# ScalarE clears two output tiles inside expert 0's branch, and the hint for the next branch is given twice per pair of tiles

## The chip, the cores and the metric

The program runs on one core of one Trainium2 chip. The metric is device time in microseconds (us) of that core, from the start to the end of one launch; the kernel before has a median of 473.15 us over three runs (471.51 to 475.03). The profiled execution is one more run of the same program. Its own time was 470.77 us; the span from its first to its last recorded instruction was 469.1 us.

Engine names follow the profile: PE is TensorE (matmuls), PEld its weight loads, ACT is ScalarE, DVE is VectorE, POOL is GpSimd, SP is SyncE. A name with a q behind it (PEq, ACTq, PEldq) is an engine's sequencer, which handles waits, registers, branches and hints.

## The reference

Two blocks are chained. The first is a retention recurrence over 4 batches, 8 heads, 768 steps and width 64; its output, laid out as 3072 tokens of 512 numbers, is the input of the second. The second is a mixture of 8 experts with one expert per token:

```python
logits = x @ w_gate
expert_idx = np.argmax(logits, axis=1)
gate_w = probs[np.arange(N), expert_idx]
...
for e in range(E):
    ...
    h = np.maximum(x_sorted[lo:hi] @ w1[e], 0.0)
    y_sorted[lo:hi] = h @ w2[e]
y = y_sorted[inv_perm]
return (gate_w[:, None] * y).astype(np.float32)
```

w1 of an expert is 512 by 1024, w2 is 1024 by 512, all in 32-bit floats. How many tokens an expert gets is known only once the gate has been computed on the chip.

## The kernel before

**The two phases.** The attention phase takes about the first 130 us of the span. It runs in 24 steps of 128 tokens, places each token in a list of its expert as it goes, and stores the rows in DRAM. It closes with the first two tiles of 128 rows of expert 0, worked on early: layer 1 of these 256 rows, and then layer 2 by `pair` (L341), a product of block matrices with 7 products instead of 8. Each of the 7 products is 4 matmuls in the source and 8 matmul records in the profile (a 32-bit matmul is recorded twice). Then the expert phase runs the experts 0 to 7 in a Python loop (L900), fully unrolled.

**The branch of an expert.** How many rows an expert has is rounded up to a multiple of 8, and each possible count has code of its own: a `tc.Switch` (L933) with 33 arms, of which one is run. PE and ACT take this branch at every expert, DVE from expert 1 on. The arm of expert 0 or 1 holds layer 1 (`layer_one`, L912, with `layer1`, L220) and layer 2 of the tiles that `pair` does not do. Layer 1 is eight groups of four matmuls into four PSUM banks in turn; ACT moves each group out with a Relu (L225), and PE may begin group 4 only when ACT has emptied the bank of group 0. Layer 2 is `layer2` (L227), its matmuls are L236 and ACT's evictions L241 to L244. From expert 2 on, layer 1 is done by `quarters1` (L291, matmuls L303), again by 7 products.

**The work between two branches.** For the experts 1 to 7, what follows the arm is straight code: `pair` on the first two tiles (matmuls L349, ACT L364 and L376, DVE L355), the scatter of the output rows and the gather of later input rows by POOL (L392, L166), weight loads by SP (L150, L155), and transposes of the next expert's rows by DVE (L209).

**The hint.** The target of a branch is computed at run time, so the kernel announces it: `fetch_ahead` (L410) gives PE and ACT a hint of which arm comes next. `pair` calls it as `then()` after its third product of seven (L370); in expert 0 and in the early pair other calls do so. At the head of each arm the framework puts a hint of its own for the jump out of the arm (recorded at L933). The arithmetic of a branch and its COMPARE_BRANCH are recorded at L989, the hint given by `fetch_ahead` at L411.

**The clearing.** Expert 0's rows beyond its real count are scattered as well (to rows out of bounds, which are dropped), so the first two tiles of `o2[0]` have to hold something. ACT clears them by two activations with scale 0.0 (L887), 128 by 512 each, placed ahead of the expert loop. `o2` lies in memory that the attention phase has used before; the first instruction that writes there waits for the last reader of each engine, among them DVE's last L355 of the early pair.

**What sets the order.** From L700 on, the order on every engine is the order of the source (`manual_schedule`), and each engine's queue is worked off in that order.

Of the kernel before, what the change touches and what calls it, by code (L numbers as in the profile page):

```python
# [17 lines left out]
AF = mybir.ActivationFunctionType  # L18
# [3 lines left out]
P = 128  # L22
# [24 lines left out]
def middle(ap, n):  # L47

    dims = [list(d) for d in ap.ap]
    return bass.AP(tensor=ap.tensor, offset=ap.offset, ap=[dims[0], [0, n]] + dims[1:])  # L50
# [3 lines left out]
def kernel(  # L54
# [11 lines left out]
    nc = tc.nc  # L66
    B, H, S, D = q.shape
    N, DM = out.shape
# [18 lines left out]
    def ps(tag, bufs, name):  # L87
        return psum.tile([P, 512], F32, tag=tag, name=name, bufs=bufs)
# [9 lines left out]
    ident = const.tile([P, P], F32, tag="ident", name="ident")  # L98
# [115 lines left out]
    def turn(xs, xT, tiles, which=range(Q * Q)):  # L214
        for _ in turns(xs, xT, tiles, which):
            pass
# [124 lines left out]
    def pair(hT, w2t, hs, ws, o, gate, then, tile_of, spare=lambda n: None, tags=None,  # L341
             late=False):

        ya, yb, yc, yd = ((ps(*tag, "yp") if tags else acc8[tag])[:, 0:DH] for tag in tags or (4, 5, 2, 3))
        g = [gate[:, i : i + 1] for i in range(2)]

        def product(y, a, b, start):
            for f in range(FH):
                nc.tensor.matmul(y, lhsT=a[:, f, :], rhs=b[:, f, :], start=start and f == 0, stop=f == FH - 1,  # L349
                                 skip_group_check=True)  # L350

        def part(name, y, i, plus):

            to = tile_of(name) if isinstance(name, str) else name
            nc.vector.scalar_tensor_tensor(out=to, in0=y, scalar=g[i], in1=plus, op0=ALU.mult, op1=ALU.add)  # L355
            return to

        A = lambda i, j: hT[:, ts(j, FH), ts(i, P)]
        B = lambda j, k: w2t[:, 0, ts(j, FH), ts(k, DH)]
        S, T = [None] + hs, [None] + ws  # L360
        m1 = [tile_of(f"m1{i}") for i in range(2)]
        product(ya, A(0, 0), B(0, 0), True)
        for i in range(2):
            nc.scalar.activation(out=m1[i], in_=ya, func=AF.Copy, scale=g[i])  # L364
        product(yb, S[2], T[2], True)
        u20, u21 = (part(f"u2{i}", yb, i, m1[i]) for i in range(2))
        spare(4)
        product(yd, S[3], T[3], True)
        u3 = part("u3", yd, 1, u21)
        then()  # L370
        spare(7)
        product(yc, S[1], T[1], True)
        part(o[:, 1, DH:DM], yc, 1, u3)
        spare(5)
        product(ya, A(0, 1), B(1, 0), False)
        nc.scalar.activation(out=o[:, 0, 0:DH], in_=ya, func=AF.Copy, scale=g[0])  # L376
        product(yd, A(1, 1), T[4], False)
        if not late:
            part(o[:, 1, 0:DH], yd, 1, u21)
        product(yc, S[4], B(1, 1), False)  # L380
        if not late:
            part(o[:, 0, DH:DM], yc, 0, u20)

        def rest():
            part(o[:, 1, 0:DH], yd, 1, u21)
            part(o[:, 0, DH:DM], yc, 0, u20)

        return rest
# [14 lines left out]
    HALF = EARLY // P  # L403
    ARMS = MOST - LEAST + 1

    def regs(e):
        return {g: nc.engines[g].value_load(arm[0:1, e : e + 1], min_val=0, max_val=ARMS - 1)
                for g in ((PE, ACT) if e < 1 else (PE, ACT, DVE))}

    def fetch_ahead(which, e):  # L410
        tc.switch_hint({g: which[g] for g in (PE, ACT)}, ARMS, label=f"job{e}")  # L411
# [381 lines left out]
    o2 = [keep2.tile([P, TC, DM], F32, tag=f"o{i}", name=f"o{i}") for i in range(2)]  # L793
# [89 lines left out]
            scatter(o2[E % 2], odst[:, ts(j, TC)], range(TC))  # L883

    if True:
        for h in range(HALF):
            nc.scalar.activation(out=o2[0][:, h, :].rearrange("p (a b) -> p a b", b=P), in_=middle(ident[:, :], DM // P),  # L887
                                 func=AF.Copy, scale=0.0)
        acc8.extend(ps(tag, n, f"p{i}") for i, (tag, n) in enumerate((("sc", 2), ("sc", 2), ("lg", 1)) + (("tr", 3),) * 3 + (("y", 2),) * 2))
        xT, xTn, rest = xTa, xT1, None  # L890
        s3 = [keep2.tile([P, 2, F // 2], F32, tag=f"s{i}", name=f"s{i}", bufs=1) for i in range(3)]
        T = [keep2.tile([P, 2, W // 2], F32, tag=f"t{i}", name=f"t{i}", bufs=1) for i in range(4)]
        hs = [keep2.tile([P, FH * P], F32, tag=f"hs{i}", name=f"hs{i}", bufs=1) for i in range(4)]
        ws = [keep2.tile([P, FH * DH], F32, tag=f"ws{i}", name=f"ws{i}", bufs=1) for i in range(4)]
        temps = [[keep2.tile([P, W // 2], F32, tag=f"q{k}{i}", name=f"q{k}{i}", bufs=1) for i in range(2)] for k in range(3)]
        turn_of = keep2.tile([P, 1], F32, tag="turn_of", name="turn_of", bufs=1)
        of_pair = dict(m10=temps[0][0], m11=temps[0][1], u20=temps[1][0], u21=temps[1][1], u3=temps[2][0])
        PLACES = (1, 1, 1, 2) * 2

        for e in range(E):  # L900
            last = e + 1 == E
            nxt = None if last else regs(e + 1)

            def hint():
                fetch_ahead(nxt, e + 1)

            hT = mp.tile([P, FT, W], F32, tag="hT", name="hT")
            if e and not last:
                xTn = xT1 if e % 2 == 0 else mp.tile([P, DT, W], F32, tag="xTs", name="xTs", bufs=1)
            xsn = xs2[(e + 1) % 2]  # L910

            def layer_one(n):  # L912
                if e < 2:
                    for f in range(FT):
                        layer1(n, xT, w1s[e], hT, f)
                    if e:
                        turn(xsn, xTn, range(TC))
                        halves_of_h(hT, hs)
                    return
                todo, counts = iter(range(Q * Q)), iter(PLACES)  # L920

                def spare():
                    k = next(counts)
                    if not last:
                        turn(xsn, xTn, range(TC), [i for _, i in zip(range(k), todo)])

                rest()
                quarters1(n, xT, w1s[e], S, T, hT, temps, spare)
                halves_of_h(hT, hs)

            if e and e + 2 < E:
                gather(xs2[e % 2], cols[e + 2][0], range(TC))
            for a in tc.Switch(which, ARMS, hint=f"job{e}"):  # L933
                n = max(STEP * (LEAST + a) - (0 if e else EARLY), STEP)
                job(n, xT, w1s[e], w2s[e], hT, o2[e % 2], cols[e][2], HALF if e else 0, lambda: None if e else hint(), layer_one)
            if e > 1:
                scatter(o2[(e - 1) % 2], cols[e - 1][1], [1, 0])
            if e == 0:
                for t in o2:
                    nc.gpsimd.memset(t[:, HALF:TC, :], 0.0)  # L940
                gather(xs2[0], cols[2][0], range(TC))
                scatter(o2[0], cols[0][1], range(HALF))
                w2s.append(weights2(homes[0], 2))
                w1s.append(weights1(homes[0], 2))
                xT, which = xTn, nxt
                continue
            halves_of_w(w2s[e], ws, by=nc.gpsimd)
            if not last:
                turn(xsn, xTn, range(TC), range(sum(PLACES) if e > 1 else Q * Q, Q * Q))
            if not last:  # L950
                halves_of_x(xTn, T)
                nc.gpsimd.tensor_copy(turn_of, T[3][:, 0, 0:1])  # L952
                S = halves_of_w1(w1s[e + 1], s3)
                xT, which = xTn, nxt
            if e + 2 < E:
                w1s.append(weights1(homes[e % 2], e + 2))
            if last:
                more = nc.values_load(over[0:1, 0:1], min_val=0, max_val=1)
            scatter(o2[e % 2], cols[e][1], range(HALF, TC))
            rest = pair(hT, w2s[e], *([x.rearrange("p (f t) -> p f t", f=FH) for x in xs_] for xs_ in (hs, ws)), o2[e % 2], cols[e][2], lambda: None if last else hint(), of_pair.get,  # L960
                        late=not last)
            if last:
                with tc.If(more > 0, preferred_fallthrough_block=False):
                    further_jobs()
                scatter(o2[e % 2], cols[e][1], [1, 0])
            if e + 2 < E:
                w2s.append(weights2(homes[e % 2], e + 2))
# [25 lines left out]
```

## Time and profile before

| what | value |
|---|---|
| median of 3 runs | 473.15 us (471.51 to 475.03) |
| profiled execution, its own time | 470.77 us |
| its span | 469.1 us, 9377 instructions |
| PE matmuls busy | 445.9 us (95%) |
| DVE, POOL, ACT busy | 301.7, 244.7, 132.2 us |
| mean granted TensorE clock | 0.984 |
| chain that ended last: PE | 62% of the span, "issue" 2% |
| L887 on ACT | 2 activations, 613 to 630 ns each, 162.0 to 163.2 us |
| branches (L989) on PE | 16, 297 ns at least, 350 in the middle, 3983 at most |

"Chain that ended last" follows the end of the run back, step by step, to what released each instruction. "Issue" in it is time in which the engine waited for nothing that the profile shows. A timeline lists an engine's instructions in order, neighbours of one kind merged, with the idle time before them in brackets and what ended it. A view of stages gives the busy time of each engine, the granted TensorE clock (PEclk) and the DMA share of each stretch.

### The profile page before, as it was taken

The numbers are of one execution on the slowest core, as the hardware profiler recorded it, in microseconds if no ns is written. First come the engines' busy times: TensorE is split into PE (matmuls) and PEld (weight loads), VectorE is DVE, ScalarE is ACT, GpSimd is POOL, SyncE is SP. The second block draws the span as 40 slices with busy tenths as digits, with TensorE's granted clock in tenths as the row PEclk, the third lists the DMA queues.
The fourth block names the chain that finished last, engine by engine and source line by source line (L and its number), as shares of the span: only waits on it lengthen the run. The fifth ranks groups of instructions, "written<-read, shape, count | busy, mean of one in ns | idle before, by whom it ended". The sixth has DMA issues, their size and how long they took to land.

```text
span 469.1 us, 9377 instructions
## 1 busy us (share of the span) xinstructions
PE 445.9 (95%) x3550; PEld 358.8 (76%) x3550; DVE 301.7 (64%) x674; ACT 132.2 (28%) x315; POOL 244.7 (52%) x192
## 2 busy tenths in 40 slices
PE   8998999999999979999999999999999989999992
PEld 4777787787667864558986995898899679699772
DVE  4468698888895995341776577378767748744410
ACT  2553444444422110221231032123223112212310
POOL 3763634450306053919842892787389289278311
PEclk9998999999999979999999999999999999999997
DMA  9999989999841095805805351481562524001001
GB/s 203 216 237 220 214 208 226 217 219 281 278 106 41 14 383 191 342 4 206 280 11 182 117 206 22 167 280 39 184 222 92 182 86 173 5 6 63 4 29 49
DMA packets 93544, 72.76 MB, mean 155 GB/s; under 512 B 53482, under 2 KB 78058, under 8 KB 93424
## 3 DMA queue, kind: packets, MB, share of 16 engines
q1 hardware_dynamic: 88160, 58.74, 44.4%
q0 software_dynamic: 5120, 12.60, 7.6%
q8 instruction: 48, 0.79, 0.7%
q14 instruction: 72, 0.59, 0.4%
q10 hardware_dynamic: 144, 0.05, 0.0%
HBM read 60.88 MB, written 14.68 MB: 161 GB/s over the span
## 4 chain that ended last, share of the span: by engine, by line
PE 62%; issue 2%; DVE 2%; ACT 1%; POOLq 0%; ACTq 0%
PE p L303 24%; PE p L349 18%; PE p L236 14%; PE p L223 6%; DVE xTa L209 1%; DVE xs L355 0%; PE yp L349 0%; POOLq L989 0%; ACT o L241 0%; ACT o L242 0%; ACT o L887 0%; DVE u L355 0%; ACT hT L225 0%; ACTq L989 0%; ACTq L887 0%
## 5 line engine op out<-in xcount | busy, mean ns | idle before, releaser
L236 PE MATMUL p<-w2t,hT 128*8 128x128 f32 (+6 forms) x496 | 66.4, 360 | 0.0
L236 PEld LDWEIGHTS p<-w2t,hT 128*8 128x8 f32 (+6 forms) x496 | 32.6, 123 | 29.5 <-issue 26.7
L209 DVE STREAM_TRANSPOSE xT<-xs 32x512 f32<-32x512 f32 x64 | 44.9, 702 | 6.0 <-issue 4.8
L392 POOL DMA_INDIRECT out_dram<-o,dst x30 | 29.9, 996 | 34.5 <-ACT o L244 18.3
L166 POOL DMA_INDIRECT xs<-x_d,src x28 | 29.3, 1045 | 26.4 <-DVE gate_e L201 14.8
L528 DVE TENSOR_TENSOR am<-sc,causal 128x512 f32<-128x512 f32 x48 | 30.7, 682 | 15.0 <-PE sc L526 15.0
L209 DVE STREAM_TRANSPOSE xTs<-xs 32x512 f32<-32x512 f32 x48 | 33.7, 702 | 9.4 <-DMA xs<-x_d,src 4.9
L485 POOL TENSOR_TENSOR qs<-q,dec 128x512 f32<-128x512 f32 x22 | 22.9, 1061 | 31.4 <-DMA q<-in_q_dram 31.4
L952 POOL COPY turn_of<-t 128x1 f32<-128x1 f32 x6 | 1.1, 183 | 71.7 <-DVE t L289 71.7
L490 POOL TENSOR_TENSOR vs<-v,dec 128x512 f32<-128x512 f32 x23 | 23.9, 1043 | 26.1 <-PE y L558 13.5
L349 PE MATMUL p<-ws,hs 128*128 128x256 f32 x168 | 37.4, 379 | 0.0
L303 PE MATMUL p<-t,w1t 128*128 128x196 f32 (+5 forms) x192 | 35.8, 329 | 0.0
L303 PE MATMUL p<-t,s 128*128 128x196 f32 (+5 forms) x192 | 35.8, 329 | 0.0
L349 PEld LDWEIGHTS p<-ws,hs 128*128 128x128 f32 x168 | 31.9, 190 | 4.3
L307 DVE TENSOR_TENSOR hT<-p,q 128x196 f32<-128x196 f32 (+5 forms) x72 | 24.8, 361 | 15.7 <-PE p L303 15.2
L265 POOL TENSOR_TENSOR ws<-w2t,ws 128x1024 f32<-128x1024 f32 x14 | 33.4, 2387 | 0.5
L265 POOL TENSOR_TENSOR ws<-w2t 128x1024 f32<-128x1024 f32 x14 | 33.2, 2369 | 0.1
L303 PEld LDWEIGHTS p<-t,w1t 128*128 128x128 f32 x192 | 32.4, 190 | 0.0
L303 PEld LDWEIGHTS p<-t,s 128*128 128x128 f32 x192 | 32.4, 190 | 0.0
L558 PE MATMUL y<-am,vs 128*64 128x128 f32 x384 | 29.6, 283 | 2.4 <-DVE am L528 2.1
L526 PE MATMUL sc<-qT,kT 64*128 64x128 f32 x384 | 28.8, 291 | 0.7 <-ACT kT L511 0.7
L355 DVE SCALAR_TENSOR_TENSOR o<-p,gate,q 128x256 f32<-128x256 f32 x21 | 10.0, 483 | 29.8 <-PE p L349 25.9
(205 smaller groups left out, 857.7 us busy)
## 6 DMA issues: line engine op xcount, KB each, us to landing
w1t<-in_moe_w_dram SPq DMA_DIRECT2D x8, 2048.0 KB, 9.0
w2t<-in_moe_w_dram SPq DMA_DIRECT2D x8, 2048.0 KB, 10.8
k<-in_k_dram SPq DMA_DIRECT2D x24, 256.0 KB, 5.6
v<-in_v_dram SPq DMA_DIRECT2D x24, 256.0 KB, 5.5
x_d<-xg SPq DMA_DIRECT2D x24, 256.0 KB, 5.0
q<-in_q_dram SPq DMA_DIRECT2D x11, 512.0 KB, 6.3
q<-in_q_dram SPq DMA_DIRECT2D x2, 256.0 KB, 3.3
out_dram<-o,dst POOLq DMA_INDIRECT x30, 3.9
```

Source lines behind the costliest of these rows:

```text
L166: nc.gpsimd.indirect_dma_start(out=xs[:, t, :], out_offset=None, in_=x_d[0:rows, :], in_offset=bass.IndirectOffsetOnAxis(ap=idx[:, t : t + ...
L209: nc.vector.transpose(xT[ts(g, L), :, 0 : n * P].rearrange("p a (t r i) -> p r t a i", r=Q, i=L)[:, r, :, :, :], xs[ts(r, L), tiles[0] : t ...
L223: nc.tensor.matmul(hp, lhsT=w1t[:, 0, dt, ts(f, P)], rhs=xT[:, dt, 0:n], start=(dt == 0), stop=(dt == DT - 1))
L236: nc.tensor.matmul(y[j * z : j * z + m, 0:c], lhsT=hT[:, f, t * P + r0 : t * P + r0 + m], rhs=w2t[:, 0, f, ts(j, c)], start=(i == 0), stop ...
L265: by.tensor_tensor(out=ws[i], in0=sums[i][0], in1=sums[i][1], op=ALU.subtract)
L303: nc.tensor.matmul(rows(y), lhsT=a(d, f), rhs=b(d), start=start and d == 0, stop=d == 1, skip_group_check=True)
L307: nc.vector.tensor_tensor(out=to, in0=rows(y), in1=rows(plus), op=ALU.add)
L349: nc.tensor.matmul(y, lhsT=a[:, f, :], rhs=b[:, f, :], start=start and f == 0, stop=f == FH - 1, skip_group_check=True)
L392: done = nc.gpsimd.indirect_dma_start(out=out[:, :], out_offset=bass.IndirectOffsetOnAxis(ap=idx[:, t : t + 1], axis=0), in_=o[:, t, :], i ...
L526: nc.tensor.matmul(sc[j][:, a, :], lhsT=kT[r, a, :], rhs=qT[r, a, :], start=True, stop=True)
L528: nc.vector.tensor_tensor(out=am[j], in0=sc[j], in1=middle(causal[:, :], HP), op=ALU.mult)
L558: nc.tensor.matmul(place_of(a, j), lhsT=vs[:, 2 * a + j, :], rhs=am[j][:, a, :], start=(c == 0), stop=True, skip_group_check=True)
```

## The change

Two edits. The two clearing activations leave the code ahead of the loop and become the first ACT instructions of every arm of expert 0's branch. And `pair` calls `then()` a second time, after its fourth product, for all pairs but the early one (which alone passes `tags`); for the last expert `then()` gives no hint. So PE and ACT each get one hint more at the experts 1 to 6.

```diff
@@ pair
         product(yc, S[1], T[1], True)
         part(o[:, 1, DH:DM], yc, 1, u3)
         spare(5)
+        if not tags:
+            then()
         product(ya, A(0, 1), B(1, 0), False)
...
@@ ahead of the expert loop
     if True:
-        for h in range(HALF):
-            nc.scalar.activation(out=o2[0][:, h, :].rearrange("p (a b) -> p a b", b=P), in_=middle(ident[:, :], DM // P),
-                                 func=AF.Copy, scale=0.0)
...
@@ layer_one
                 if e < 2:
+                    for h in range(0 if e else HALF):
+                        nc.scalar.activation(out=o2[0][:, h, :].rearrange("p (a b) -> p a b", b=P),
+                                             in_=middle(ident[:, :], DM // P), func=AF.Copy, scale=0.0)
                     for f in range(FT):
                         layer1(n, xT, w1s[e], hT, f)
```

## The prediction

> **What bounds the kernel now.** I read the page first: PE is busy for 95% of the span, so a change pays only where PE stands still or runs slowly. The second part of the page shows where: of its 40 slices (11.7 us each) the 15th, 164 to 176 us, alone has a PE digit of 7, but for the end, and there the clock row shows a 7 too.
>
> ```profile
> PE 445.9 (95%) x3550; PEld 358.8 (76%) x3550; DVE 301.7 (64%) x674; ACT 132.2 (28%) x315; POOL 244.7 (52%) x192
> PE   8998999999999979999999999999999989999992
> ...
> PEclk9998999999999979999999999999999999999997
> ```
>
> Then the chain that ended last, in order of time (start, duration, what). It is PE nearly throughout; these are the places where it leaves PE:
>
> ```profile
> 161.90 0.03 ACTq L887
> ...
> 162.04 0.34 ACT o L887
> ...
> 163.18 0.06 ACTq L989
> 163.25 4.70 issue
> 167.95 0.04 ACTq L933
> ...
> 168.09 0.27 ACT hT L225
> 168.36 0.04 issue
> 168.40 6.57 PE p L223 x32
> ...
> 382.43 1.59 issue
> ```
>
> Read it forwards: ACT clears two tiles (L887), branches at 163.18, and for 4.70 us nothing happens before it stands in the arm of expert 0 (L933). PE waits for that. Near the end PE itself loses 1.59 us at expert 6's branch. Next the timelines of ACT and of PE around expert 0:
>
> ```profile
> 157.88 0.47 ACT L376 ACTIVATE xs<-yp,gate_e 128x256 f32<-128x256 f32 x1 [7.39 <-PE yp L349]
> 162.04 1.15 ACT L887 ACTIVATE o<-ident 128x512 f32<-128x512 f32 x2 [3.69 <-DVE at_e L188]
> 168.09 0.71 ACT L225 ACTIVATE hT<-p 128x104 f32<-128x104 f32 x4 [4.90 <-issue]
> ```
>
> ```profile
> 161.13 3.78 PE L223 MATMUL p<-xTa,w1t 128*128 128x104 f32 x32
> 168.40 6.57 PE L223 MATMUL p<-xTa,w1t 128*128 128x104 f32 x32 [3.49 <-ACT hT L225]
> 174.80 7.03 PE L236 MATMUL p<-w2t,hT 128*104 128x512 f32 x16
> ```
>
> ACT is free at 157.88 but stands in L887's waits until 161.92, for DVE's last L355 (161.41 + 0.48). Only then does it branch. PE does four groups, finds the first bank still full, idles 3.49 us, and the same 32 records then take 6.57 us instead of 3.78. The stages say why:
>
> ```profile
> 165.00:170.00 5.00, 1.60 (x7) 1.60 (x8) 4.91 (x8) 0.71 (x4) 2.86 (x3) 0.74 0.99 356
> 170.00:175.00 5.00, 5.00 (x28) 4.98 (x27) 4.83 (x10) 0.77 (x3) 2.68 (x3) 0.58 1.04 407
> ```
>
> The last three columns are PEclk, DMA share and GB/s: the clock falls to 0.74 and 0.58 (it is 1.00 in the stretches around them), while the DMA engines are full with the weights of expert 1 (issued by SP at 162.02). Last, PE's own branches, expert 6's and expert 3's:
>
> ```profile
> L989 PEldq COMPARE_BRANCH  x1: 3377/3377/3377, 380.4 to 380.4; - x1
> ```
>
> ```profile
> L989 PEldq COMPARE_BRANCH  x1: 391/391/391, 260.5 to 260.5; - x1
> ```
>
> [...] ACT 4.70 us, PE 3.38 us, and 16 KB instruction packets on queue q8. [...] 3.49 us idle, then records spaced 213 ns instead of 111. [...] In this trace PE's sequencer branches 2 to 3.7 us before its last matmul ends, so a short fetch is hidden.
>
> **Part 1, the clearing.** Nothing is removed: 2 activations (1.15 us together) and their waits move from ahead of ACT's branch to behind it; every arm of expert 0 gets them ahead of L225. No DMA moves with them. What moves forward on ACT is the register load and the branch. After L376 at 157.88 the sequencer needs about 0.8 us for them (184.86 to 185.67 at expert 1), so it branches near 158.75. The fetch: 4.70 us with full DMA engines; at the experts 2 to 7 the same gap on ACT is 2.4 to 3.3 us. In 155 to 160 us the DMA engines carry nothing (the weights start at 162.02 and stay there, since SP waits for DVE), so I take 2.5: ACT is in the arm at 161.25, against 167.95. There it meets the same wait for DVE (161.92) and a new one for PE's last early product (about 161.3), passes at 162.25, clears until 163.4, and empties the four banks by 164.0 (4 evictions took 0.71). PE needs the first bank at 164.75. If the fetch took 4.7 all the same, ACT would arrive at 163.5, clear until 164.8, and PE would wait some 0.3 us[...]. So both ends of the unknown fetch give nearly the same.
>
> Gain: idle 3.49, plus slow records 6.57 - 3.78 = 2.79, together **6.3 us**.
>
> What is late next? PE reaches expert 1 at about 175.4 instead of 181.67. There it needs: the rows xT (DVE's 16 transposes from 163.00 for 11.47, so 174.5); w1 of expert 1 (issued at 162.02, landing after 10.6 us by the DMA view, 172.6); its own branch, which took 3.98 us at 176.70 and ended 0.6 us before it was needed, with the DMA engines as full then as they will be at 170.3. All fit, by 0.9, 2.8 and about 0.5 us. [...] DVE's jump now comes ahead of the other seven of its eight target instructions (L189 on), which may cost the 0.6 us gap seen after that jump at 163.06 and bring xT to 175.1, still in time; POOL's and SP's jumps (33 to 38 ns) now come ahead of the first scatter and of the load of w1, which wait for DVE anyhow. I charge 0.2 us for these thin margins: **6.1 us** is left. Behind that, the gathers of expert 2 stay where they are, with DVE's transposes at 180.77 to 192.2 and DVE's next need of ACT's last hT moving from 203.4 to about 197.2; everything else (POOL's sums, weight loads released by PE) follows PE, so the gain is carried to the end.
>
> **Part 2, the second hint.** Six sequencer instructions (3 MOVE, FUSED_REGOPS, ALU_OP, hint) on PE and on ACT at the experts 1 to 6. On PE they are about 0.09 us apart, 0.55 us per hint; PE's sequencer is well ahead of its matmuls there, and the first hint shows no idle time behind it, so: nothing; without that cover 6 x 0.55 = 3.3. On ACT both hints come back to back (no ACT work lies between), under a wait of 2.5 us or more for L376: nothing. ACT's branch costs 2.4 us or more with one hint already, and I expect the second to change nothing.
>
> What can it gain on PE? Of the six branches behind a pair, five took 0.30 to 0.40 us and one 3.38, and that one cost 1.59. Why that one? Between two branches PE has 129 instructions (112 weight loads and matmuls, 4 waits, 6 for the hint, 3 for the register, 4 for the branch). In the trace the hint brings a q8 packet within 1.6 to 3.9 us, except at expert 6, where the packet comes 0.48 us after the branch has begun. [...] The second hint makes the distance 135, and every later position shifts by 6 more per expert. By my count expert 6's branch then [...] (gain 1.59), but expert 2's [...] misses: its branch is 3.06 us ahead of PE's last matmul (220.86 against 223.92), so a fetch of 3.4 to 4.5 and 0.26 of start cost 0.6 to 1.7. Experts 3 and 4 get part of a miss, within their 2.8 to 3.0 us of cover. Bounds: if the second hint cures all, -1.6; if it cures nothing and expert 2 misses, +1.7. I take -1.6 + 0.9 = **-0.7**.
>
> **Sum.** 6.1 + 0.7 = 6.8 us off the profiled 470.77, so 464.0 there. The median of the runs shown is 2.4 us above the profiled one; the same 6.8 off it gives **466.3**.
>
> **Rivals.** (B) *The shift of positions does more harm.* Two or three branches miss by 1 to 2 us each: 6.1 - 3.5, so 470.5. For it: the one miss seen looks positional. Against: a cover of 2 to 3.7 us. (C) *A new wait takes over.* PE comes early to expert 1 and waits for the branch fetch or for xT, or ACT is late there after its own two fetches (2.84 and 4.56 us, slack 1.9), and half of the gain goes: 470. For it: thin margins in a stretch with full DMA engines. Against: every one of them fits by the numbers. (D) *Slower: the second hint cancels the fetch that the first began,* and all six branches of PE miss. At 3.4 us per fetch they cost 0.6, 0.6, 0.9, 1.4, 1.6 and 0 with covers of 3.06, 3.03, 2.77, 2.22, 2.05 and 3.65, 5.1 in all; at the 3.98 seen at expert 1 about 8.7. Less the 1.6 paid already that is 7.1 against 6.1: 474.2. It decides from a fetch of about 3.85 us. Against: 3.38 at expert 6, and the second hint still comes some 3 us before the branch. That the clearing brings nothing would need ACT still to arrive past 167, against an idle DMA; I count it in C.
>
> **How the numbers follow.** A 0.70, B 0.13, C 0.12, D 0.05. A's own range is 464 to 468.4. Leaving out D and the worst of B and C, and adding the spread of the three runs below A, the range is 463.5 to 471.0. A difference of 1% (4.7 us) is about what this measurement can tell from none. Faster by over 1% is A and a little of B and C, 0.76; within 1% the rest of B and C and a little of D, 0.20; slower by over 1%, 0.04.
>
> **What would show it.** Right: L225 of expert 0 begins near 163.5 on ACT, PE has no wait for it between 161 and 170, PEclk is 1.00 there, L223's second 32 records take 3.8, and expert 1's L223 starts near 175.4. Part 2: PE's branch records at L989 behind the pairs; I expect expert 6's at 0.3 to 0.4 and expert 2's over 2. Wrong: an ACT fetch that ends past 165, a wait on DVE or a DMA at expert 1, or idle PE ahead of L303 at several experts.

## The result, and the profile after

The changed kernel has a median of 467.96 us (465.16 to 469.15, six runs), the kernel before on the same chip 475.19 us (471.51 to 476.35, six runs): a ratio of 0.9854, with a 95% interval from 0.9811 to 0.9897. The profiled execution took 468.13 us, its span is 466.4 us.

The dip is gone from the row of PE, and from the row of the clock, at the 15th slice (one slice is 11.7 us). The 7 that is new at the 11th slice lies in the attention phase, which the change does not touch:

```profile
PE   8899999989799999999999999999989999999992
...
PEclk9999999999989999999999999999999999999998
```

In this execution the attention phase ended 1.78 us later than in the one before: PE began expert 0's L223 at 162.91 and not at 161.13. So the two traces are compared from there on. The timelines of ACT and of PE around expert 0:

```profile
159.66 0.47 ACT L378 ACTIVATE xs<-yp,gate_e 128x256 f32<-128x256 f32 x1 [7.39 <-PE yp L349]
163.99 1.15 ACT L914 ACTIVATE o<-ident 128x512 f32<-128x512 f32 x2 [3.86 <-DVE at_e L188]
165.05 0.38 ACT L225 ACTIVATE hT<-p 128x104 f32<-128x104 f32 x2
```

```profile
162.91 7.36 PE L223 MATMUL p<-xTa,w1t 128*128 128x104 f32 x64
170.11 7.03 PE L236 MATMUL p<-w2t,hT 128*104 128x512 f32 x16
177.81 4.52 PE L223 MATMUL p<-xT,w1t 128*128 128x392 f32 x13 [0.67 <-DVE dst L195]
```

L223 of expert 0 is now one row of 64 records in 7.36 us, with no idle time inside. Before it was two rows of 3.78 and 6.57 us with 3.49 us between them. ACT's sequencer, by the view of the branch line and of the arm's first line:

```profile
L991 ACTq COMPARE_BRANCH  x1: 62/62/62, 160.4 to 160.4; - x1
```

```profile
L935 ACTq BRANCH_PREFETCH_HINT  x1: 36/36/36, 163.0 to 163.0; - x1
```

ACT branches at 160.43, right behind its last eviction, and stands in the arm at 163.01. The gap is 2.52 us, and all of it now lies inside the wait for DVE that ACT has to sit out in any case. The stages (the last three columns are PEclk, DMA share and GB/s) show the full clock while the DMA engines are about as full as before (shares of 0.86 and 1.01 against 0.99 and 1.04):

```profile
165.00:170.00 5.00, 5.00 (x47) 5.00 (x46) 4.90 (x8) 1.71 (x8) 3.87 (x4) 1.00 0.86 307
170.00:175.00 5.00, 5.00 (x15) 2.15 (x14) 4.91 (x8) 0.26 (x1) 1.60 (x2) 1.00 1.01 393
```

From PE's start on expert 0 to its start on expert 1 it took 20.54 us before and 14.90 now: 5.64 us gained. From there to the end of the span it took 287.4 us before and 288.6 now: 1.2 us are given back. One place of that is seen in the branches of PE (start in the last column, duration in ns ahead of it): expert 1's, expert 5's, expert 6's, expert 7's.

```profile
L991 PEldq COMPARE_BRANCH  x1: 4791/4791/4791, 172.3 to 172.3; - x1
...
L991 PEldq COMPARE_BRANCH  x1: 3572/3572/3572, 336.8 to 336.8; - x1
...
L991 PEldq COMPARE_BRANCH  x1: 388/388/388, 378.6 to 378.6; - x1
...
L991 PEldq COMPARE_BRANCH  x1: 2041/2041/2041, 413.9 to 413.9; - x1
```

Expert 6's long branch (3.38 us before) is short. Expert 5's, 0.30 us before, is long in its place, and the chain of waits loses as much there as it lost at expert 6 before:

```profile
329.88 9.09 PE p L349 x42
338.97 1.61 issue
340.58 4.46 PE p L303 x24
```

### The profile page after: what moved, and what is told of

Read it like the earlier page. It is cut to its first block, busy times and chain, and to the rows that moved or that the text cites. A ratio compares the mean times of both kernels' runs of the same rounds, so it can differ in the third digit from the quotient of the medians.

```text
span 466.4 us, 9449 instructions
## 1 busy us (share of the span) xinstructions
PE 443.3 (95%) x3550; PEld 354.6 (76%) x3550; DVE 295.1 (63%) x674; ACT 130.5 (28%) x315; POOL 244.0 (52%) x192
## 4 chain that ended last, share of the span: by engine, by line
PE 59%; DVE 5%; issue 1%; ACT 0%; POOLq 0%; DVEq 0%
PE p L303 24%; PE p L349 18%; PE p L236 13%; PE p L223 5%; DVE xT L209 2%; DVE xTa L209 1%; DVE xs L355 0%; PE yp L349 0%; POOLq L991 0%; ACT o L241 0%; ACT o L242 0%; DVE u L355 0%; DVE hT L307 0%; DVE two L189 0%; DVE dst L195 0%
## 5 line engine op out<-in xcount | busy, mean ns | idle before, releaser
L560 PEld LDWEIGHTS y<-am,vs 128*64 128x64 f32 x384 | 22.9, 140 | 7.5 <-DVE am L530 4.4
```

Source lines behind the costliest of these rows:

```text
L560: nc.tensor.matmul(place_of(a, j), lhsT=vs[:, 2 * a + j, :], rhs=am[j][:, a, :], start=(c == 0), stop=True, skip_group_check=True)
```

## The experiments

The theory after the result: part 1 alone made the gain, since ACT now fetches its arm while the DMA engines are idle; the second hint only moves PE's later instructions on and so moves the miss from one expert to another. The rivals: the second hint matters; the fetch was slow for another reason than the full engines; the clearing work itself counts.

The table holds what is read from all runs. "0 to 1" is the time from PE's start on expert 0's L223 to its start on expert 1's, "rest" from there to the end of the span; then the durations of PE's branches of the experts 2 to 7, in us. The ratio is to the kernel before on the same chip; where there is none, the kernel ran once. Every time in the last three columns comes from one profiled execution of its kernel.

| kernel | median us | ratio (95%) | 0 to 1 | rest | branches of the experts 2 to 7 |
|---|---|---|---|---|---|
| before | | | 20.54 | 287.4 | .40 .39 .31 .30 **3.38** .31 |
| changed | 467.96 | 0.9854 (0.9811 to 0.9897) | 14.90 | 288.6 | .53 .29 .30 **3.57** .39 **2.04** |
| changed_again | 469.72 | one run | 14.95 | 289.6 | .39 .30 .30 **3.21 3.46 1.97** |
| clear_only | 468.23 | 0.9895 (0.9844 to 0.9945) | 14.71 | 289.1 | .39 .30 .31 .40 **3.26** .30 |
| hint_only | 474.68 | 1.0006 (0.9984 to 1.0029) | 20.70 | 288.8 | .40 **2.70 1.58 3.51 1.69 1.84** |
| filler | 469.00 | one run | 14.80 | 288.8 | .39 **3.07 1.75 3.30** .39 **2.19** |
| three | 469.31 | 0.9918 (0.9890 to 0.9947) | 14.88 | 288.3 | .49 .29 .30 .39 **3.26** .39 |
| placed | 467.13 | 0.9872 (0.9811 to 0.9933) | 14.61 | 288.1 | .40 .30 .30 .39 **2.10** .39 |
| weights_late | 469.56 | 0.9918 (0.9879 to 0.9956) | 15.26 | 289.8 | .40 .30 .30 .39 **3.26** .30 |
| clear_pool | 469.13 | 0.9908 (0.9879 to 0.9938) | 14.73 | 289.2 | .40 .30 .31 .39 **3.56** .39 |
| late_only | 474.06 | one run | 16.44 | 291.5 | .39 **3.24 2.85 1.77 3.10 3.64** |
| early | 469.86 | 0.9904 (0.9869 to 0.9940) | 16.24 | 288.7 | .39 .31 .40 .39 **3.32** .30 |
| early_one | 475.45 | 1.0030 (1.0009 to 1.0051) | 20.52 | 293.0 | .31 .39 .31 .30 **3.20** .39 |

### One part alone: clear_only and hint_only

clear_only is the changed kernel without the second `then()` in `pair`. hint_only keeps that and puts the clearing back ahead of the loop:

```diff
 # clear_only, against the changed kernel
-        if not tags:
-            then()
```

```diff
 # hint_only, against the kernel before
         spare(5)
+        if not tags:
+            then()
```

> The clearing moved as in the change, one hint in the pair as before. Theory (early branch): the whole gain sits here. ACT branches 2 to 3 us before the weights of expert 1 fill the DMA engines, its gap behind the branch of expert 0 is about 2.5 us and not 4.7, PE has no wait in expert 0's L223 and TensorE's clock stays at 1.00 there; expert 1's first matmul comes 5.5 to 6 us earlier against the end of the pair of the early tiles. With no second hint PE's instructions stand where they stood before, so expert 6's branch still takes about 3.4 us and costs 1.6. Time: 5 to 6 us under the kernel before, equal to the changed kernel within 1.5 us. Rival (the second hint matters): at least 2 us slower than the changed kernel.

> The clearing ahead of the branch as before, the second hint as in the change. Theory (position): the second hint only moves PE's later instructions on by six per expert. Expert 6's branch is short (0.4 us), expert 5's takes about 3.5 us and costs 1.6, expert 7's some 2 us that matmuls hide; the time is that of the kernel before within 1 us. Rival 1 (the second hint is what brings the code in): all branches from expert 2 on are short, and the time is 1.6 us lower. Rival 2 (it breaks off the first fetch): several branches take 3 us or more, and the time is 3 us higher or more. ACT's wait of 3.5 us and the slow clock at expert 0 are unchanged under all three.

Measured: clear_only has a ratio of 0.9895, hint_only one of 1.0006, and its interval leaves no more than 0.3% either way. So the gain is part 1's. In clear_only PE has no wait at expert 0, and expert 1 starts 14.71 us after expert 0. Its branch of expert 6 takes 3.26 us, as without the second hint it should:

```profile
L989 PEldq COMPARE_BRANCH  x1: 3260/3260/3260, 376.9 to 376.9; - x1
```

hint_only has long branches where the change has them (expert 5: 3.51, expert 7: 1.84) and further ones at the experts 3, 4 and 6 (2.70, 1.58, 1.69), which the changed kernel's trace does not show. Of them all only expert 5's costs PE much (1.36 us idle), as the others end while matmuls are still queued.

### Is it the hint, or six more instructions? filler

In the place of each second hint PE loads a register twice with a value that nothing uses: six sequencer records, as a hint has.

```diff
-            then()
+            then(2)
...
-lambda: None if last else hint()
+lambda k=0: None if last else [nc.tensor.value_load(arm[0:1, e : e + 1], min_val=0, max_val=ARMS - 1) for _ in range(k)] if k else hint()
```

> As the changed kernel, but in the place of each second hint PE runs two register loads of a value that nothing uses: six sequencer records, as many as a hint has, and no hint. ACT gets one hint per expert. Theory (position): PE's branches come out as with the second hint: expert 5's about 3.5 us with 1.6 us of idle time ahead of L303, expert 6's 0.4, expert 7's about 2. Rival (the hint itself does it): they come out as with one hint, expert 6's about 3.4 and all others 0.3 to 0.4.

```profile
L991 PEldq COMPARE_BRANCH  x1: 3304/3304/3304, 337.7 to 337.7; - x1
...
L991 PEldq COMPARE_BRANCH  x1: 386/386/386, 379.4 to 379.4; - x1
...
L991 PEldq COMPARE_BRANCH  x1: 2192/2192/2192, 414.8 to 414.8; - x1
```

Without any second hint the experts 5, 6 and 7 come out as in the changed kernel: 3.30, 0.39, 2.19 us. So it is the added instructions that move the miss, and not the hint. The experts 3 and 4 (3.07 and 1.75) were not expected to be long; they come out as in hint_only. Since filler has no second hint, these long branches do not show that a second hint breaks off the first.

### Other places and other numbers: three, placed, late_only, early

`three` gives the second hint at the experts 1 to 3 only. `placed` gives one hint per expert, but five more in the pair of expert 5, which moves PE's later instructions on by 30. `late_only` keeps only the second hint, `early` moves the single hint ahead of the first product. All have the clearing inside the branch.

```diff
 # three: the second then() passes 3
+lambda k=E: None if last or e > k else hint()
 # placed: then(2) after spare(5), then(3) after the next product
+lambda k=0: None if last else [hint() for _ in range(k * (e == 5) if k else 1)]
```

> As the changed kernel, but the second hint is given only at experts 1 to 3 (the branches of experts 2 to 4). Theory (position): PE's instructions move on by 6, 12 and then 18 for every later expert. [...] experts 2 to 5 and 7 take 0.3 to 0.5 us, expert 6 at most 2.5 us, which its matmuls hide. The idle time of 1.6 us ahead of a L303 is gone, so the time is about 1.6 us below the changed kernel, some 7 us below the kernel before. Rival (each branch needs its own second hint): experts 5, 6 and 7 have one hint as before, expert 6's takes 3.4 us, and nothing is gained over the changed kernel.

> The clearing moved and one hint per expert as before the change, but five more hints in the pair of expert 5 alone, so that PE's instructions move on by 30 ahead of the branch of expert 6 and stand as in the kernel before at the experts 2 to 5. Theory (position): the branches of experts 2 to 5 take 0.3 to 0.4 us as in the kernel before, expert 6's about 0.4 as in the changed kernel, which moved it on by 30 too; expert 7's up to 2 us, hidden; no idle time ahead of a L303 over 0.6 us by a branch. Time 0.5 to 1.5 us below the clearing moved alone. Rival (the place does not decide): expert 6's branch takes 3.3 us again.

> As the changed kernel, but of the two hints only the second one is given: one hint per expert as before, some 1.6 us later in the pair, and PE's instructions stand where they stood before. Theory (position): as in the kernel before, expert 6's branch takes about 3.3 us and the others of the experts 2 to 7 take 0.3 to 0.5. Rival (the later hint cures a fetch that was given too early): expert 6's takes 0.4 and those of experts 5 and 7 too. Rival 2 (a later hint comes too late): several branches take 1 to 3 us.

> The clearing moved and one hint per expert, but given ahead of the first product of the pair of tiles, some 5 us earlier than in the kernel before; no instruction is added, so PE's branches stand where they stood before. Theory after the late hint alone (a hint has to stand far enough ahead in the instructions; given past some place it is served only at the branch): expert 6's branch falls from 3.3 us to about 0.4 like all others from expert 2 on, no idle time by a branch ahead of a L303, 0.5 us or more below the clearing moved alone. Rival (the place of the branch decides and not that of the hint): expert 6's takes 3.3 us again. Rival 2 (a hint given too early is lost): several branches take 3 us.

Measured. three: expert 5's branch is short, as expected with 18 instructions more ahead of it in place of 24, but expert 6's takes 3.26 us and not the 2.5 at most that I had given it. PE idles 0.56 us there, so the 1.6 us were not gained in full. placed: expert 6's takes 2.10 us, between the 0.4 expected and the rival's 3.3, and all of it is hidden. late_only: nothing is shifted, and yet in its one trace five of six branches take 1.77 to 3.64 us:

```profile
L992 PEldq COMPARE_BRANCH  x1: 3241/3241/3241, 261.5 to 261.5; - x1
...
L992 PEldq COMPARE_BRANCH  x1: 3638/3638/3638, 419.4 to 419.4; - x1
```

So the place of the hint matters too: 1.6 us later, it does not bring the code in time. This falls against the theory that the branch's own place decides. But the opposite doesn't hold: in early the hint comes earlier and expert 6's branch still takes 3.32 us. Both late_only and early also start expert 1 some 1.5 to 1.7 us later than clear_only, with 2.0 to 2.2 us of idle time there: the jump out of expert 0's arm takes 2.11 and 2.12 us in them and 0.59 and 0.76 in the changed kernel and clear_only. The packet with the code behind the jump begins only 0.37 and 0.26 us ahead of it in them, and 1.79 and 1.62 us ahead in the other two. The moved hint does not explain this: the instructions that PE runs up to this jump are the same in early, late_only and clear_only. The cause is open, and chance is not excluded.

### The same kernel again: changed_again

> The changed kernel once more, unaltered, to see whether its branches repeat: expert 5's about 3.5 us and expert 7's about 2, all others from expert 2 on 0.3 to 0.5, if the place of the instructions alone decides; other values at the experts 3, 4 or 6, where the run with the second hint alone differed, if chance has a part.

The experts 5 and 7 repeat (3.21 and 1.97 us), the experts 3 and 4 are short again, expert 6 does not repeat: 3.46 us against 0.39. So the place of the instructions is enough to explain the experts 5 and 7, and at expert 6 the outcome varies from run to run.

### Was the fetch slow because the DMA engines were full? weights_late

The clearing stays ahead of the branch, as before the change. But the load of expert 1's weights is held back until ACT is in expert 0's arm: ACT writes one element per partition of the weight tile there, which the load then overwrites.

```diff
                 if e < 2:
+                    if e == 0:
+                        nc.scalar.activation(out=w1s[1][:, 0, 0, 0:1], in_=ident[:, 0:1], func=AF.Copy, scale=0.0)
...
             if e == 0:
+                nc.sync.dma_start(w1s[1], w1v[:, ds(1, 1), :, :])
+                nc.sync.dma_start(w2s[1], w2v[:, ds(1, 1), :, :])
```

> The order of the kernel before (clearing ahead of the branch, one hint), but the load of expert 1's weights is held back: ACT writes one element of the tile w1t inside the branch of expert 0, and SP issues the load after that, so that ACT's fetch meets DMA engines that carry no weights. Theory (the fetch was slow because the engines were full): ACT branches at about 163.2 as before, its gap is about 2.5 us and not 4.7, it empties the first bank near 166, PE idles 1.2 us and not 3.5[...] and the second 32 records of L223 take 3.8 us and not 6.6. The weights come some 4 us later, which costs expert 1 up to 1 us. Time: 4 to 5 us under the kernel before. Rival (the fetch takes 4.7 us whatever the engines do): gap and idle time as before, and a time within 1 us of the kernel before.

The timelines of PE and ACT, and the stage:

```profile
162.18 3.78 PE L223 MATMUL p<-xTa,w1t 128*128 128x104 f32 x32
166.61 3.82 PE L223 MATMUL p<-xTa,w1t 128*128 128x104 f32 x32 [0.65 <-ACT hT L225]
```

```profile
163.09 1.15 ACT L887 ACTIVATE o<-ident 128x512 f32<-128x512 f32 x2 [3.69 <-DVE at_e L188]
166.21 0.20 ACT L915 ACTIVATE w1t<-ident 128x1 f32<-128x1 f32 x1 [1.97 <-issue]
```

```profile
160.00:165.00 5.00, 5.00 (x36) 4.57 (x35) 4.73 (x17) 1.15 (x2) 0.12 (x1) 1.00 0.02 5
```

ACT branches as late as before, 164.2. With a DMA share of 0.02 around it, the gap is 1.83 us and not 4.70. PE idles 0.65 us, the clock stays at 1.00, and the second 32 records take 3.82 us. The rival, a fetch that takes 4.7 us whatever the engines do, is out. Expert 1 starts 15.26 us after expert 0, so 5.3 of the 5.6 us come with the DMA engines emptied and the branch as late as before. The ratio is 0.9918, or 3.9 us of 473, just under the 4 to 5 expected.

### Does the clearing work count? clear_pool

```diff
-        for h in range(HALF):
-            nc.scalar.activation(out=o2[0][:, h, :] ...
+        nc.gpsimd.memset(o2[0][:, 0:HALF, :], 0.0)
```

> One hint; the clearing is taken off ACT altogether: GpSimd clears the two tiles (one memset of about 0.9 us) behind its scatters, and nothing is added to the branch of expert 0. Theory (the wait ahead of the branch is what cost): ACT branches near 158.7 as with the clearing inside the branch, stands in the arm at about 161.3, PE has no wait in expert 0's L223, and the time is that of the clearing moved alone, 5 to 6 us under the kernel before, within 1 us of it. Rival (the 1.15 us of clearing work counts also inside the branch): about 1 us below the clearing moved alone. Rival 2 (GpSimd's clearing delays its gathers): 1 us or more above it.

0 to 1 takes 14.73 us, against 14.71 in clear_only. The 1.15 us of clearing cost nothing that can be seen inside the branch, and GpSimd's memset (0.98 us) nothing where it stands. What cost was only what stood ahead of the branch: the wait.

### The hint of expert 1 earlier: early_one

Expert 1's branch is the longest of all (4.4 to 5.0 us in the kernels with the early branch), and it meets the weights of expert 1 in the DMA engines (a DMA share of 1.03 to 1.06). So in early_one, PE and ACT get that hint at the beginning of expert 0's arm and not ahead of its last tile.

```diff
                 if e < 2:
+                    if e == 0:
+                        hint()
```

> As the early hint, and in the arm of expert 0 the hint for expert 1 is given at its beginning, on PE near 161 us, before the weights of expert 1 fill the DMA engines, and no longer ahead of its last tile. Theory (the branch of expert 1 is slow since its fetch meets full engines): that branch falls from 4.5 to 4.8 us to under 1, and the 0.5 us that PE idles ahead of expert 1 goes, unless the rows xT, whose last row numbers come at the same moment, hold it in its place; 0 to 0.5 us gained. Rival (the code brought in early is lost on the way, or the hint is not served): the branch takes 4.5 us as before and nothing is gained.

The profiled execution took 480.75 us, 5 us above the median, so its whole time is not read here, only the jump out of expert 0's arm, then expert 1's branch, and what follows at once.

```profile
L994 PEldq COMPARE_BRANCH  x1: 6422/6422/6422, 173.1 to 173.1; - x1
...
L994 PEldq COMPARE_BRANCH  x1: 4567/4567/4567, 180.6 to 180.6; - x1
```

Expert 1's takes 4.57 us as ever, and the jump ahead of it takes 6.42 and not 2.12 as in early. In the records of instruction packets there is one at 165.18, behind the two hints that come 0.55 us apart at the head of the arm, and no further one until 177.07, 4 us after the jump has begun. In changed_again there are two in the same stretch, at 163.24 and 169.14. So an early hint for the branch after next did not bring its code in, and what the jump needed was missing too. PE idles 6.29 us ahead of expert 1, the clock is at 0.50 for 6.83 us from 184.21 on, and L223 of expert 1 takes 23.86 us in place of 21.30. The slow clock is not this trace's alone: the mean clock of the 20 runs is 0.976 to 0.988, that of early's six 0.988 to 0.993. The ratio is 1.0030, against 0.9904 without this edit: about 6 us lost.

## Why the prediction was right, and where not

**Part 1, the ACT branch: right.** Shifted by the 1.78 us of the later start, I expected the branch at 160.5, the arm at 163.0, and the end of the clearing at 165.2; they came at 160.43, 163.01 and 165.14. PE did not wait, and the clock did not fall. weights_late shows the reason: the same late branch, with idle DMA engines, takes 1.83 us. The wait behind the branch is 4.70 us beside a full transfer (a DMA share of 0.94 over it), against 1.83 and 2.52 us without one (0.02 around it and 0.04 over it). The packet records show which part of the wait grows. ACT's packet of code begins 3.07 us after its branch in the kernel before, 0.88 in the changed kernel and 0.18 in weights_late; from there ACT needs 1.64 us to stand in the arm in all three. So the full engines delay the start of the fetch and not the rest of it. Why weights_late, with engines as empty as in the changed kernel, starts it sooner is open.

**Part 1, the margins at expert 1: mechanism right, size too small.** I charged 0.2 us in all. PE idled 0.67 us ahead of expert 1, in changed_again 0.71, in clear_only 0.48. The step that was mis-sized is PE's branch: I took 3.98 us from before, "with the DMA engines as full then as they will be", and it took 4.79. They were not as full then. The stages of the two branches, before and after, have DMA shares of 0.43 and 1.04:

```profile
176.69:180.67 3.98, 3.98 (x10) 1.54 (x10) 0.00 (x0) 0.00 (x0) 0.00 (x0) 1.00 0.43 156
```

```profile
172.27:177.06 4.79, 4.79 (x12) 1.69 (x10) 4.62 (x12) 0.00 (x0) 3.05 (x3) 1.00 1.04 404
```

Here too it is the start of the fetch that moved: PE's packet begins 1.52 us into the branch before and 2.38 now, and the branch ends 2.46 and 2.42 us after that. The margin was read too wide as well. Where the branch holds PE, PE starts 0.69 to 0.75 us after its end; before it was 0.99, so some 0.3 us were to spare and not the 0.6 of the prediction. The timeline names DVE's L195 as the releaser, and L195 does end at 177.61. But PE was not waiting for it: its branch ends at 177.06, and the five waits behind it are passed one by one.

```profile
L223 PEldq EVENT_SEMAPHORE  x5: 51/51/51, 177.3 to 177.7; - x5
```

Each takes 51 ns and they stand 106 ns apart, so none of them held. In placed and clear_pool PE starts expert 1 even 0.11 and 0.21 us before L195 ends. The rows xT were in time, as predicted: DVE's last transpose of them ends at 176.24, and 174.5 + 1.78 is 176.3. So rival C happened, at about a tenth of the gain and not a half.

**"With DVE's transposes at 180.77 to 192.2": wrong.** They came at 185.64, which is 3.1 us later even after the shift:

```profile
185.64 11.45 DVE L209 STREAM_TRANSPOSE xTs<-xs 32x512 f32<-32x512 f32 x16 [8.03 <-issue]
```

DVE branches for expert 1 at 179.32 and stands in the arm at 185.17, a gap of 5.80 us against 2.75 before. In all the kernels that start expert 1 early it is 5.6 to 6.9, and in hint_only, which does not, 2.82. The DMA share over the gap is 1.05 now and was 0.32. I had not counted DVE's branch among what now meets full DMA engines.

**"So the gain is carried to the end": wrong by about 1.2 us.** The rest takes 288.1 to 289.8 us in the kernels that start expert 1 early, with or without a second hint (early_one and late_only left out), against 287.4 before. New small waits stand there: 0.27 us for DVE's hT at expert 2, 0.56 us at expert 4. Before and hint_only have no wait at expert 4, the other eleven traces have one of 0.41 to 0.80. It can't be put down to the earlier start alone, for early_one has it too (0.60) and starts expert 1 no earlier; what the eleven share is DVE's long gap at expert 1. And hint_only, without that wait, has a rest of 288.8 us all the same, with 1.36 us at expert 5 and 0.57 at expert 2. Before's 287.4 is the shortest rest of all 13 traces. How much of the 1.2 us is the change and how much is chance of that one profile can't be told.

**Part 2: the failed step.** The prediction had expert 6's branch short (0.3 to 0.4 us) and a miss at expert 2 (over 2 us), by a count of instruction positions that was my estimate and that no trace showed. Expert 6's was short (in one trace of two), but expert 2's never missed, in any trace: 0.31 to 0.53 us. Expert 5's missed, 3.57 us, and cost 1.61 us, as much as expert 6's had cost. So the net of part 2 is nothing that can be seen (hint_only has a ratio of 1.0006), and not the 0.7 us that the sum has. The idea behind it, that the shift and not the hint acts, is borne out by filler (3.30, 0.39 and 2.19 us at the experts 5, 6 and 7 without any second hint). The positions that I derived from one trace were not: no count of mine places all the misses of the table, and changed_again shows that one of them is not fixed by position at all. That the second hint cures all is excluded by the changed kernel and hint_only, which still have long branches; that it breaks off the first, by filler, which has the long branches without it.

**The sum.** Predicted 6.8 us. The medians say 7.2 (475.19 less 467.96), the traces 5.64 less 1.2, which is 4.4. Against hint_only, the other trace with the late branch, it is 6.0: from PE's start on expert 0 to the end 309.55 us there and 303.51 in the changed kernel.

Two things on record bear on this. First, the trace of before is a quick one. Its execution took 470.77 us with a mean clock of 0.984, while of the 77 runs of that kernel that stand beside the experiments, on three chips, the 38 with a clock of 0.987 or less took 472.58 to 477.09 us. Second, the prediction counted the slow records, 2.79 us, as lost in every run. 25 of the 77 have a mean clock of 0.990 or more. By my estimate that leaves no room for them: the 6.83 us at a clock of 0.50 in the trace of before, with the 3.2 us at that clock that every trace has at its end at the least, make 0.989 or less of 470 us. So the gain is smaller in some runs than in others.

The other kernels with the early branch (clear_only, three, placed, clear_pool) have ratios of 0.987 to 0.992, which is 3.9 to 6.1 us of 474, with 0.45 to 0.76 us lost at expert 6's branch in all of them but placed. All their intervals overlap that of the changed kernel. So the size of the gain is 4 to 7 us. That the median came so near to the predicted 466.3 is in part luck: part 2 gave nothing, part 1 gave less in the trace, and the forecast stood on a median of 473.15 us for the kernel before, which became 475.19 with three runs more.

**What stays open.** Which instruction positions make PE's branch miss, and why a hint given some 1.6 us later (late_only) no longer brings the code in time. In every miss the packet of code begins late, 1.1 us ahead of the branch to 1.0 us behind its start; what holds it back is not in the traces. No kernel here is shown to beat the changed one: placed has the lowest median, 467.13 us, within the interval of the changed kernel, and clear_only does the same with half of the edit.

## What to carry to other kernels

Behind ACT's branch of expert 0, full DMA engines put off the start of the code's packet here (3.00 to 3.07 us behind the branch, against 0.18 to 1.10 us with them idle), so look at what the DMA engines do when each engine reaches its branch. An instruction with a late wait, placed ahead of the branch, pushed it into the next load of weights (the load issued at 162.02, ACT's branch at 163.18); moving that instruction behind the branch did away with PE's wait of 3.49 us, and holding the load back left 0.65 us of it. Six instructions more per expert moved PE's long branch from expert 6 (3.38 us in before) to the experts 3, 4, 5 and 7 in filler (1.75 to 3.30 us); count what covers each long branch (2 to 3.7 us of queued matmuls here) before work goes into it. Where one engine is made earlier, look for the other engines' branches that now fall into the full stretch (DVE's gap at expert 1: 5.80 us against 2.75). And read the clock of all runs before a slow stretch of one trace is counted in full.

## What the runs showed of the hardware

- The gap behind ACT's branch of expert 0 was 1.83 us with a DMA share of 0.02 (weights_late), 2.4 to 2.6 with the engines idle (a share of 0.04 in the changed kernel) in the ten traces that branch between 159 and 163 us, and 4.5 to 4.7 with them full (hint_only, before; a share of 0.94 in before). ACT's packet of code began 0.18, 0.87 to 1.10, and 3.00 to 3.07 us after the branch, and ACT stood in the arm 1.5 to 1.7 us after that in all 13 traces. One hint or two made no difference to ACT (2.4 to 3.7 us at the experts 2 to 7 in all kernels).
- PE's branch of expert 1 took 3.9 and 4.0 us at a DMA share of 0.41 and 0.43 (hint_only, before) and 4.4 to 5.0 us at 1.03 to 1.06 (the other eleven traces). DVE's gap there was 2.75 and 2.82 us at shares of 0.32 and 0.34, and 5.6 to 6.9 at 1.01 to 1.05.
- PE's branches of the experts 2 to 7 took either 0.29 to 0.53 us or 1.6 to 3.6 us. All of the long ones, those of expert 1 and the slow jumps out of an arm ended 2.3 to 2.9 us after a packet of instructions began, whatever the DMA share (at expert 1, 2.46 us at a share of 0.43 in before and 2.42 at 1.04 in the changed kernel).
- In the one kernel that gave a hint for a later branch 0.55 us behind the hint for the next one, the next one took 6.42 us (early_one).
- PE's pause of 3.49 us was followed by 32 records in 6.57 us, one of 3.34 us (hint_only) by the same in 6.87, one of 0.65 us (weights_late) in 3.82. Pauses of 2.01 and 2.21 us ahead of expert 1 (early, late_only) left its L223 at 21.30 us, as in the changed kernel; one of 6.29 us (early_one) made it 23.86.
